# First stage of a Fourier-mixing kernel: the two ends of the first index as 64x32 tiles side by side, outputs at a pitch of 56 columns

## The chip, the cores and the metric

The kernel runs on one core of a Trainium2 chip. The metric is the device time of one execution in microseconds (us). Before the change three runs took 1851.91, 1852.71 and 1855.34 us; their median is 1852.71.

## The reference

The reference takes `x` of shape 8 x 3008 x 256 (batches, sequence, features) and two weight matrices, 256 x 2048 and 2048 x 256, all float32. It computes the real part of a two-dimensional Fourier transform of each batch and sends the 24064 rows of the result through a small network:

```python
X = np.fft.fft(x, axis=1)
X = np.fft.fft(X, axis=2)
a = X.real.reshape(8 * 3008, 256)
h = a @ w_in
g = h * (1.0 / (1.0 + np.exp(-1.702 * h)))
out = g @ w_out
```

## The kernel before, in words

The transform over the sequence of 3008 = 47 x 64 is done in two stages. The transform over the features is folded into the first weight matrix (`wcs`), so that it costs no step of its own. The rest, by far the largest part, is the network: products of 64-column halves on TensorE, with the activation between them on ScalarE and sums on VectorE and GpSimd. The steps of the network (`steps`, a batch, a block of four, a half and a pair of hidden blocks each) are written out in one loop, and what has to be done for the next batch is put between them by a table, `extra`: `at(t, fn, ...)` runs `fn` at the end of step `t`. The order on every engine is the order of this program; nothing rearranges it.

For batch b + 1 the table holds, while batch b runs through the network: the load of `x` into `xt` (`load_x`); `fold1` on GpSimd, which adds and subtracts mirrored rows and, at its first call, puts the two ends of the first index (0 and 32 of the 64 residues) into a tile `e` of their own; four calls of `mix1`, the first stage; after each of them two calls of `spill`, which write the result to `Td` in DRAM; `fill`, which reads it back with other rows; and `stage2`, which multiplies it with the matrices of the second stage in tiles of 64x32.

`mix1(b, m)` uses the array of TensorE in four quarters of 64 rows by 64 columns. Quarter (r, c) reads 47 partitions of `xt` from partition 64 r on and writes 64 partitions of a PSUM bank `ps[r]` from partition 64 c on. In each call every quarter has two matmuls of 256 columns, one per i. Each writes 48 useful rows: 24 frequencies, of each a part 0 and a part 1 in turn (NM = 48); the weights are read as windows of 64 columns at a pitch of 48, so that the last 16 rows come from the next matrix and are not used.

The one matmul with jj = 0, in quarter (0, 0) of the call with m = 0, is special. The ends have only one part each: part 0 from index 0, part 1 from index 32. It is made of four matmuls, two pieces of the columns (0 to 128 and 129 to 255) by two parts. The weights of part 0 have zeros in the columns of part 1 and the other way round, and the second of each pair adds to the first in the same 64 rows. The four quarters' matmuls are issued in an order that takes, each time, the quarter with the least work so far (`had`); an ordinary matmul counts 2 in it and one of the four end matmuls 1.

After `mix1` ScalarE copies both banks into `xt` (`mixed`, the second bank in the next step), and the spills take 48 partitions from partition 64 c on. The first batch has a first stage of its own (`mix_first`), so that `mix1` runs for seven batches.

Of the kernel before, what the change touches and what calls it, by code (L numbers as in the profile page):

```python
# [27 lines left out]
F32 = mybir.dt.float32  # L28
# [6 lines left out]
NA, NB = 47, 64  # L35
NJ = NB // 2
NM = 48
ENDS = 0, NJ, NJ + 1, NJ + 2
PIECES = (0, 32), (32, NA)
NU, NG = 2, 12  # L40
# [6 lines left out]
def view(ap, offset, *dims):  # L47
    return bass.AP(ap.tensor, ap.offset + offset, [list(d) for d in dims])
# [6 lines left out]
def kp(u, a):  # L55

    n, i = a // 4, 2 * (a % 4) + u
    return 8 * n + i if n else 7 - i


def tables(S, D):

    assert S == NA * NB and D == 256
    H = D // 2
    ks = np.array([kp(u, a) for a in range(NG) for u in range(NU)])
    s = NB * np.arange(NA)[:, None, None] + np.arange(NB)[None, :, None]
    angle = 2.0 * np.pi * ((s * ks) % S) / S
    cos, sin = np.cos(angle), np.sin(angle)
    w1 = np.zeros((NA, NJ + 3, NG * NU, 2))
    w1[:, 1:NJ, :, 0], w1[:, 1:NJ, :, 1] = cos[:, 1:NJ], sin[:, 1:NJ]  # L70
    e0, o0, e1, o1 = ENDS
    w1[:, e0, :, 0], w1[:, o0, :, 0], w1[:, e1, :, 1], w1[:, o1, :, 1] = cos[:, 0], sin[:, 0], cos[:, NJ], sin[:, NJ]


    w0 = np.zeros((128, NJ + 1, NG * NU, 2))
    low, high, back = w0[0:2 * NA:2], np.zeros((NA, NJ + 1, NG * NU, 2)), NJ - np.arange(1, NJ)
    low[:] = w1[:, :NJ + 1]
    high[:, 1:NJ, :, 0], high[:, 1:NJ, :, 1] = cos[:, NJ + back], -sin[:, NJ + back]
    high[:, e0, :, 1], high[:, o0, :, 1] = cos[:, NJ], -sin[:, NJ]
    w0[33:33 + 2 * NA:2] = high  # L80
    sign = np.ones((128, 4))
    sign[33:33 + 2 * NA:2] = -1.0

    c, q = np.divmod(np.arange(NJ), 16)
    m2 = []
    for jj in np.where(c, 16 + q, np.where(q, 16 - q, 0)), 4 * (q // 2) + 2 * (q % 2) + c:
        j, k2 = jj[:, None], np.arange(NB)[None, :]
        beta = 2.0 * np.pi * ((j * k2) % NB) / NB
        m = np.zeros((NU, 2, NJ, 2, NB))
        m[:, 0, :, 0], m[:, 1, :, 0] = np.cos(beta), -np.sin(beta)  # L90
        m[:, 0, :, 1], m[:, 1, :, 1] = np.sin(beta), np.cos(beta)
        m[:, :, 0, 0] = m[:, :, 0, 1] = np.stack([np.ones(NB), 1.0 - 2.0 * (np.arange(NB) % 2)])
        m2.append(m)
    rot = np.zeros((NU, 2, NJ, NU, 2, NJ))
    for i in range(NU):
        for n in range(NJ):
            rot[i, 0, n, i, 1, n], rot[i, 1, n, i, 0, n] = (1.0, -1.0) if n else (0.0, 0.0)
        rot[i, 0, 0, i, 0, 0] = rot[i, 1, 0, i, 1, 0] = 1.0

    m, d = np.arange(D)[:, None], np.arange(H)[None, :]  # L100
    phi = 2.0 * np.pi * ((m * d) % D) / D
    cd = np.stack([np.cos(phi), -np.sin(phi)], 1)
    cd[:, 1, 0] = 1.0 - 2.0 * (np.arange(D) % 2)
    cd = cd.reshape(2, H, 2, H).transpose(1, 0, 2, 3)
    small = [t.reshape(128, -1) for t in (*m2, rot, cd)]
    pad = 64 - NM
    w1 = np.pad(w1.reshape(NA, -1), ((0, 128 - NA), (0, pad)))
    w0 = np.concatenate([w0.reshape(128, -1), np.zeros((128, pad)), sign], 1)
    return np.concatenate([w0, w1], 1).astype(np.float32), np.concatenate(small, 1).astype(np.float32)

# [2 lines left out]
def kernel(ctx: ExitStack, tc, x, w_in, w_out, tab1, tab2, out):  # L113
    nc = tc.nc
    B, S, D = x.shape
# [6 lines left out]
    const = ctx.enter_context(tc.tile_pool(name="const", bufs=1, space=SB))  # L122
# [11 lines left out]
    Tk = nc.dram_tensor("Tk", (B * NBLK * NF, 1), F32, kind="Internal").ap()  # L134
    Td = [nc.dram_tensor(f"Td{b}", (NG * 128, D), F32, kind="Internal").ap() for b in range(B)]

    w1 = const.tile([128, (NJ + 3) * NM + 64 - NM], F32, tag="w1", name="w1")
    small = const.tile([128, 4 * NB + 128 + 4 * H], F32, tag="small", name="small")
    m2f, m2 = (small[:, i * 2 * NB:(i + 1) * 2 * NB].rearrange("p (c n) -> p c n", c=2) for i in range(2))
    rot = small[:, 4 * NB:4 * NB + 128]  # L140
# [21 lines left out]

    def mat(w, jj, rows):

        return w[rows, jj * NM:jj * NM + 64]

    spare = ["b0", "b1", "b2", "o2", "o3", "o4"]

    def bank(name, tag=None):
        if tag is None:  # L170
            tag = spare.pop(0)
            spare.append(tag)
        if tag in ("o0", "o1"):
            return o_banks[int(tag[1])]
        return (rest if tag[0] == "o" else psp).tile([128, 512], F32, tag=tag, name=name)
# [11 lines left out]
    xt = xp.tile([128, NJ, D], F32, tag="x", name="xt")  # L187
# [20 lines left out]
    e0 = {}  # L208
# [24 lines left out]
    def mix1(b, m):  # L233

        ps = [bank("ps1") for _ in range(2)]
        queues = {}
        for i in (2 * m, 2 * m + 1):
            for r in range(2):
                for c in range(2):
                    rows, o = slice(64 * r, 64 * r + NA), ps[r][64 * c:64 * c + 64, i % 2 * D:(i % 2 + 1) * D]  # L240
                    jj, todo = 4 * i + 2 * r + c, queues.setdefault((r, c), [])
                    if jj:
                        todo.append((2, o, mat(w1, jj, rows), xt[rows, 31 - (2 * i + c), :], not todo, True))
                        continue
                    for k, c0, c1 in ((0, 0, H + 1), (1, H + 1, D)):
                        for part in range(2):
                            todo.append((1, o[:, c0:c1], mat(w1, ENDS[k + 2 * part], rows), e0[b][:, part, c0:c1], not todo,
                                         part == 1))

        had = {key: 0 for key in queues}  # L250
        while any(queues.values()):
            key = min((key for key in queues if queues[key]), key=lambda key: (had[key], key))
            size, o, w, rhs, first, end = queues[key].pop(0)
            had[key] += size
            nc.tensor.matmul(o, lhsT=w, rhs=rhs, start=first, stop=end, skip_group_check=True)  # L255

        waiting.append((m, ps[1]))
        mixed(m, 0, ps[0])
# [3 lines left out]
    def mixed(m, r, ps):  # L262
        nc.scalar.copy(free(xt[:], (4 * m + r) * D, [2 * D, 2], [1, D]), free(ps[:], 0, [D, 2], [1, D]))
# [6 lines left out]
    def at_rows(first, at, *dims):  # L270
        one = xt[first:first + 1]
        return bass.AP(one.tensor, one.offset + at * D, [[2 * xt[:].ap[0][0], NM]] + [list(d) for d in dims])

    def load_first(k):

        lo, apart = 4 * k, (28 - 8 * k) * D
        nc.sync.dma_start(out=at_rows(0, lo, [apart, 2], [1, 4 * D]), in_=view(x, lo * D, [NB * D, NM], [apart, 2], [1, 4 * D]))

    def load_mirror(k):

        parts = ((1, 4), (28, 32)) if k == 0 else ((4 * k, 4 * k + 4), (28 - 4 * k, 32 - 4 * k))
        for lo, hi in parts:
            nc.scalar.dma_start(out=at_rows(33, lo, [D, hi - lo], [1, D]),
                                in_=view(x, (NB - lo) * D, [NB * D, NM], [-D, hi - lo], [1, D]))
        if k == 0:
# [50 lines left out]

    def spill(b, c, q):

        nc.sync.dma_start(out=view(Td[b], (16 * c + 4 * q) * D, [NJ * D, NM], [1, 4 * D]),
                          in_=xt[64 * c:64 * c + NM, 4 * q:4 * q + 4, :].rearrange("p q d -> p (q d)"))  # L340

    def fill(b, a0=0, a1=NG):
        if a0 == 0:
# [504 lines left out]
    for lo, hi in (28, 32), (24, 28), (20, 24), (8, 12), (12, 20):  # L848
# [8 lines left out]
                      in_=view(tab1, 0, [tab1.shape[1], 128], [28 * NM, 2], [1, ends]))  # L857
# [101 lines left out]
    for b in range(B):  # L959
# [5 lines left out]
        if b + 1 < B:  # L965
            folds, groups, filled = PLANS[min(b, 1)]
            for c in range(NCH):
                for part in range(2):
                    at(t0 + folds[2 * c + part], fold1, b + 1, c, part, nc.gpsimd)
                if c % 2:  # L970
                    k = t0 + groups[c // 2]
# [18 lines left out]
    for t in range(n + LAG):  # L990
        if t < NP:
# [32 lines left out]
            if t == NP - 1:  # L1024
                doubled(NP)
                middle(NP + 1)
        else:
            after, special = (any(fn in (mix1, stage2) for fn, _ in extra.get(k, ())) for k in (t - 1, t))
            if t < n:
                begin(t, 1)  # L1030
# [81 lines left out]
```

## Time and profile before

| | |
|---|---|
| median of 3 runs | 1852.71 us |
| the profiled execution | 1851.27 us, its span 1849.5 us |
| granted TensorE clock | 0.999 |
| busy: TensorE, VectorE, ScalarE, GpSimd | 99%, 80%, 62%, 54% |
| mean of the DMA engines | 57 GB/s |

The span reaches from the first instruction to the last; the execution's own time also has what lies around it, here 1.8 us. PE is TensorE's matmuls, PEld its weight loads, DVE VectorE, ACT ScalarE, POOL GpSimd and SP the engine that issues most transfers. In the profile each float32 matmul is two instructions MATMUL, called passes below. A form such as 47*64 gives the rows and columns of the array that are used; the groups give minimum, median and maximum in ns. The timeline's columns are the start in us, the time that the merged instructions cover in us, the engine, the line and the operation, output and inputs, the form, and how many were merged. Matmuls are pipelined, so the covered time of neighbours overlaps.

### The profile page before, as it was taken

What the parts mean: (1) busy time and instruction counts of PE and PEld (TensorE: products, weight loads), DVE (VectorE), ACT (ScalarE), POOL (GpSimd) and SP (SyncE); (2) the same over time, 40 slices, a digit from 0 to 9 for tenths busy, and PEclk for the clock granted to TensorE, in tenths of its full rate; (3) what the DMA queues carried; (4) which work ended last, traced back from release to release, by engine and by line L of the source; (5) the groups of instructions that cost most, each with busy time, mean ns of one, the idle gap of its engine ahead of it and who ended that gap; (6) DMA issues with size and microseconds to landing.
All of it is one profiled execution on the core that took longest, in us unless ns stands there. A gap on an engine that the chain in (4) does not pass through costs nothing.

```text
span 1849.5 us, 55986 instructions
## 1 busy us (share of the span) xinstructions
PE 1835.5 (99%) x23722; PEld 1411.0 (76%) x23722; DVE 1485.5 (80%) x1928; ACT 1148.6 (62%) x2241; POOL 1001.1 (54%) x1053
## 2 busy tenths in 40 slices
PE   8999999999999999999999999999999999999998
PEld 5677777777777777777777777777788777778776
DVE  6988778887888778877788778878888788878875
ACT  5666656666666666666665666666655666656663
POOL 4786456554556546565365544656446654444442
PEclk9999999999999999999999999999999999999999
DMA  8721341214211151211502115121241112100111
GB/s 285 178 61 34 87 65 28 55 32 103 44 48 40 33 112 29 60 33 48 109 13 71 33 48 97 22 72 26 71 73 23 35 26 56 30 19 13 23 19 24
DMA packets 149706, 105.31 MB, mean 57 GB/s; under 512 B 106057, under 2 KB 130665, under 8 KB 148896
## 3 DMA queue, kind: packets, MB, share of 16 engines
q1 hardware_dynamic: 146624, 99.68, 24.0%
q8 instruction: 187, 3.06, 0.7%
q10 hardware_dynamic: 2832, 2.05, 0.5%
q14 instruction: 63, 0.52, 0.1%
HBM read 64.41 MB, written 48.05 MB: 61 GB/s over the span
## 4 chain that ended last, share of the span: by engine, by line
PE 88%; DVE 8%; DMA 2%; ACT 1%; issue 1%; POOL 0%; SPq 0%; DVEq 0%; ACTq 0%; POOLq 0%
PE x L184 32%; PE o L184 25%; PE low L684 23%; PE o L684 4%; PE ps L255 2%; DVE big L650 2%; PE ps L365 1%; DVE big L622 1%; DVE big L604 1%; DVE big L786 1%; DVE big L648 1%; DVE big L646 1%; DMA xt<-in_x_dram 1%; DMA Td<-big 1%; DVE big L804 0%
## 5 line engine op out<-in xcount | busy, mean ns | idle before, releaser
L615 POOL TENSOR_TENSOR big<-big 128x256 f32<-128x256 f32 (+1 forms) x376 | 357.9, 952 | 797.0 <-ACT big L607 694.5
L184 PE MATMUL x<-pq,wcs 128*64 128x256 f32 (+1 forms) x6016 | 776.8, 376 | 1.0 <-ACT x L585 0.4
L184 PE MATMUL o<-big,wo 128*64 128x256 f32 (+1 forms) x4800 | 629.0, 375 | 0.6 <-issue 0.6
L184 PEld LDWEIGHTS x<-pq,wcs 128*64 128x64 f32 x6016 | 421.9, 137 | 175.9 <-issue 15.3
L184 PEld LDWEIGHTS o<-big,wo 128*64 128x64 f32 x4800 | 348.0, 137 | 145.9 <-issue 1.0
L597 ACT ACTIVATE g<-x 128x512 f32<-128x512 f32 (+1 forms) x376 | 221.8, 590 | 379.9 <-PE x L184 378.6
L604 DVE TENSOR_TENSOR big<-g,x 128x512 f32<-128x512 f32 (+1 forms) x376 | 250.8, 667 | 186.5 <-ACT big L600 186.4
L616 POOL TENSOR_TENSOR big<-big 128x256 f32<-128x256 f32 (+1 forms) x376 | 399.6, 1063 | 0.0
L585 ACT ACTIVATE x<-nb,af 128x256 f32<-128x256 f32 (+1 forms) x752 | 353.0, 469 | 69.1 <-DVE pq L372 55.9
L684 PE MATMUL low<-big 128*64 128x128 f32 (+1 forms) x5888 | 386.1, 270 | 0.0
L684 PEld LDWEIGHTS low<-big 128*64 128x64 f32 x5888 | 341.0, 137 | 27.9
L600 ACT ACTIVATE big<-x 128x512 f32<-128x512 f32 (+1 forms) x376 | 219.2, 583 | 123.5 <-PE x L184 113.6
L646 DVE TENSOR_TENSOR big<-big 128x1024 f32<-128x1024 f32 (+1 forms) x184 | 234.1, 1272 | 65.2 <-PE low L684 41.4
L607 ACT ACTIVATE big<-big 128x512 f32<-128x512 f32 (+1 forms) x376 | 231.7, 616 | 37.2 <-DVE big L604 35.4
L684 PE MATMUL low<-big,wo 128*64 128x128 f32 (+1 forms) x2944 | 224.8, 271 | 1.4 <-DVE big L650 0.7
L648 DVE TENSOR_TENSOR big<-big 128x512 f32<-128x512 f32 (+1 forms) x184 | 177.1, 963 | 15.9
L650 DVE TENSOR_TENSOR big<-big 128x512 f32<-128x512 f32 (+1 forms) x184 | 185.4, 1007 | 0.0
L684 PEld LDWEIGHTS low<-big,wo 128*64 128x64 f32 x2944 | 175.4, 137 | 6.4 <-DVE big L650 2.9
L622 DVE TENSOR_TENSOR big<-big 128x512 f32<-128x512 f32 (+1 forms) x188 | 140.7, 748 | 3.3 <-POOL big L615 3.3
L623 DVE TENSOR_TENSOR big<-big 128x512 f32<-128x512 f32 (+1 forms) x188 | 135.6, 721 | 6.5
L684 PEld LDWEIGHTS o<-big,wo 128*64 128x64 f32 x1472 | 94.3, 137 | 24.3
L684 PE MATMUL o<-big,wo 128*64 128x128 f32 (+1 forms) x1472 | 112.2, 270 | 0.0
(97 smaller groups left out, 1144.6 us busy)
## 6 DMA issues: line engine op xcount, KB each, us to landing
out_dram<-os SPq DMA_DIRECT2D x284, 64.0 KB
t<-Td SPq DMA_DIRECT2D x22, 512.0 KB
Td<-xt SPq DMA_DIRECT2D x56, 192.0 KB
xt<-in_x_dram SPq DMA_DIRECT2D x14, 512.0 KB
xt<-Xr SPq DMA_DIRECT2D x14, 512.0 KB
nb<-Nd SPq DMA_DIRECT2D x23, 256.0 KB
out_dram<-os SPq DMA_DIRECT2D x96, 56.0 KB
Xr<-in_x_dram SPq DMA_DIRECT2D x7, 752.0 KB
```

The lines of the kernel that those rows point to most:

```text
L184: nc.tensor.matmul(out[c0:c0 + 64], lhsT=lhs[:, c0:c0 + 64], rhs=rhs, skip_group_check=True, **how)
L585: nc.scalar.activation(x[:, i * 256:i * 256 + n], nbt[b, blk][:, hh * 256:hh * 256 + n], ACTF.Copy, scale=af1[:, f:f + 1])
L597: nc.scalar.activation(two(g[:], n), two(xb[t][:], n), ACTF.Copy, scale=2.0)
L600: nc.scalar.activation(front(t), two(xb[t][:], width(t)), ACTF.Gelu_apprx_sigmoid)
L604: nc.vector.tensor_tensor(back(t), two(gt.pop(t)[:], n), two(xb.pop(t)[:], n), op=ALU.subtract)
L607: nc.scalar.activation(back(t), back(t), ACTF.Gelu_apprx_sigmoid)
L615: eng.tensor_tensor(right(t, S1, n), left(t, A21, n), right(t, A22, n), op=ALU.add)
L616: eng.tensor_tensor(left(t, S3, n), left(t, A11, n), left(t, A21, n), op=ALU.subtract)
L646: nc.vector.tensor_tensor(free(big[:], SUM, *both_), free(big[:], from11 + w, *twice), free(big[:], from11, [at_right(t, 0) + w - from11, ...
L648: nc.vector.tensor_tensor(s2, a11, s1, op=ALU.subtract)
L650: nc.vector.tensor_tensor(s4, a12, s2, op=ALU.subtract)
L684: nc.tensor.matmul(o, lhsT=lhs, rhs=rhs, start=first_in, stop=(p == NP - 2), skip_group_check=True)
```

## The change

`PITCH` is 56: the 24 columns of part 0 come first, then 8 of zeros, then the 24 of part 1, so that part 1 begins at row 32 of a quarter. The table `w1` is laid out in this way, and windows of 64 columns are read at the new pitch. The four end matmuls take 32 columns each: part 0 writes rows 0 to 31 of the quarter, part 1 rows 32 to 63, and none adds to another. In `had` an ordinary matmul counts 4 and one of the end matmuls 1. A spill becomes two transfers of 24 partitions, one for each part, to the same places in `Td`.

```diff
+PITCH = 32 + NM // 2
...
-    w1 = np.pad(w1.reshape(NA, -1), ((0, 128 - NA), (0, pad)))
+    apart = np.zeros((NA, NJ + 3, PITCH))
+    apart[:, :, :NM // 2], apart[:, :, 32:] = w1[..., 0], w1[..., 1]
+    w1 = np.pad(apart.reshape(NA, -1), ((0, 128 - NA), (0, 64 - PITCH)))
...
-        return w[rows, jj * NM:jj * NM + 64]
+        return w[rows, jj * PITCH:jj * PITCH + 64]
...
                     if jj:
-                        todo.append((2, o, mat(w1, jj, rows), xt[rows, 31 - (2 * i + c), :], not todo, True))
+                        todo.append((4, o, mat(w1, jj, rows), xt[rows, 31 - (2 * i + c), :], not todo, True))
                         continue
                     for k, c0, c1 in ((0, 0, H + 1), (1, H + 1, D)):
                         for part in range(2):
-                            todo.append((1, o[:, c0:c1], mat(w1, ENDS[k + 2 * part], rows), e0[b][:, part, c0:c1], not todo,
-                                         part == 1))
+                            at = ENDS[k + 2 * part] * PITCH + 32 * part
+                            todo.append((1, o[32 * part:32 * part + 32, c0:c1], w1[rows, at:at + 32], e0[b][:, part, c0:c1],
+                                         k == 0, True))
...
-        nc.sync.dma_start(out=view(Td[b], (16 * c + 4 * q) * D, [NJ * D, NM], [1, 4 * D]),
-                          in_=xt[64 * c:64 * c + NM, 4 * q:4 * q + 4, :].rearrange("p q d -> p (q d)"))
+        for k in range(2):
+            at = 64 * c + 32 * k
+            nc.sync.dma_start(out=view(Td[b], (16 * c + 4 * q + NJ * k) * D, [2 * NJ * D, NM // 2], [1, 4 * D]),
+                              in_=xt[at:at + NM // 2, 4 * q:4 * q + 4, :].rearrange("p q d -> p (q d)"))
```

The tile for `w1` in SBUF grows from 1696 to 1968 columns.

More of the change, by code (lines that the diff above doesn't have):

```diff
@@ L135 @@
     Td = [nc.dram_tensor(f"Td{b}", (NG * 128, D), F32, kind="Internal").ap() for b in range(B)]
-    w1 = const.tile([128, (NJ + 3) * NM + 64 - NM], F32, tag="w1", name="w1")
+    w1 = const.tile([128, (NJ + 3) * PITCH + 64 - PITCH], F32, tag="w1", name="w1")
     small = const.tile([128, 4 * NB + 128 + 4 * H], F32, tag="small", name="small")
```

## The prediction

> **What bounds the kernel now.** I read the page first: busy shares, then the chain.
>
> ```profile
> PE 1835.5 (99%) x23722; PEld 1411.0 (76%) x23722; DVE 1485.5 (80%) x1928; ACT 1148.6 (62%) x2241; POOL 1001.1 (54%) x1053
> ...
> PE 88%; DVE 8%; DMA 2%; ACT 1%; issue 1%; POOL 0%; SPq 0%; DVEq 0%; ACTq 0%; POOLq 0%
> ```
>
> TensorE (PE) is busy 99% of 1849.5 us and carries 88% of the chain that ended last; in the view of waits its largest single wait is 2.7 us, at the start. So a change of TensorE's own time is passed on one to one, and I look for nothing else before that is settled. A matmul here is float32 and shows in the trace as two passes, each with a weight load (PEld) of its own.
>
> Next the instructions that write the first stage's PSUM tile `ps`:
>
> ```profile
> L255 PE MATMUL ps<-xt,w x434: 375/376/428, 120.2 to 1541.3; 47*64 47x256 f32 x145
> L255 PE MATMUL ps<-e,w x56: 266/269/322, 120.2 to 1429.0; 47*64 47x129 f32 x28, 47*64 47x127 f32 x28
> L365 PE MATMUL ps<-t,small x1536: 268/269/296, 31.9 to 1728.0; 64*32 64x128 f32 x192
> ```
>
> The change touches the 56 passes that read `e` (28 matmuls, four in each of seven batches) and their neighbours. Durations of single passes overlap, so I take times from starts. The timeline of one block with the ends (batch 2, m = 0), with the last matmul before and the first after it:
>
> ```profile
> 305.70 0.60 PE L184 MATMUL o<-big,wo 128*64 128x256 f32 x4
> 306.24 0.32 PE L255 MATMUL ps<-e,w 47*64 47x129 f32 x1
> 306.24 0.44 PE L255 MATMUL ps<-xt,w 47*64 47x256 f32 x3
> ...
> 306.73 0.27 PE L255 MATMUL ps<-e,w 47*64 47x127 f32 x1
> 306.73 0.38 PE L255 MATMUL ps<-xt,w 47*64 47x256 f32 x2
> 306.84 0.27 PE L255 MATMUL ps<-e,w 47*64 47x127 f32 x1
> ```
>
> and one without ends (m = 1), followed by the same work:
>
> ```profile
> 342.93 1.09 PE L255 MATMUL ps<-xt,w 47*64 47x256 f32 x16
> 343.95 0.65 PE L184 MATMUL x<-pq,wcs 128*64 128x256 f32 x4
> ```
>
> Three things to see. The four quarters of the array run side by side: an end and three ordinary passes start together at 306.24. The quarter with the ends is a chain of its own, one 128-column pass each 0.107 us (306.73, 306.84) beside ordinary 256-column passes at twice that. And the block with ends takes 1.44 us from its first start to the next work (306.24 to 307.68), the one without 1.02 (342.93 to 343.95): the ends cost 0.42 us in each of seven batches, 2.95 us in all. The reason is in the counts: quarter (0,0) has eight end passes of 0.107 and two ordinary ones of 0.215, 1.29 us; the others four of 0.215, 0.86 us.
>
> Last, what a change of tile shape costs:
>
> ```profile
> 307.38 0.38 PE L255 MATMUL ps<-xt,w 47*64 47x256 f32 x1
> 307.68 0.41 PE L184 MATMUL x<-pq,wcs 128*64 128x226 f32 x2
> ```
>
> ```profile
> 29.40 0.59 PE L335 MATMUL warm<-wcs 128*128 128x512 f32 x1
> 29.92 0.65 PE L184 MATMUL psw<-wst,small 128*64 128x512 f32 x2
> ```
>
> From 64x64 to 128x64 the next start comes 0.30 us after a pass that streams for 0.215: 0.09 lost. From 128x128 to 128x64, where only the width differs, 0.52 after a pass of 0.43: 0.09 again. I find 0.092 to 0.096 at every change of shape in the trace, stage 2's 64x32 tiles included. Behind each the first pass is longer by its weight load, which was not taken ahead as within one shape: 0.05 us for 64 columns (0.267 against 0.216), 0.03 for 32 (0.134 against 0.107).
>
> **The change, part by part.**
>
> *The ends.* Four matmuls of 64x64 become four of 64x32. Parts 0 and 1 no longer add into the same 64 rows but write rows 0 to 31 and 32 to 63. Side by side they need the time of two matmuls, four passes instead of eight: 0.43 us off quarter (0,0). That two 64x32 tiles of one quarter run together is shown by stage 2, where eight such tiles start within 0.05 us.
>
> *The order.* With the sizes 4 and 1 the sort by work done gives, for m = 0: one end; the three ordinary matmuls of the other quarters; three ends; four ordinary ones. By the shapes: 64x32, 64x64, 64x32, 64x64, three changes inside a block that before had none; those on entry and exit stay. A change between 64x64 and 64x32 is not in the trace. Its price lies between nothing (a change of tile within a shape: the next start 0.006 us later) and 0.094 plus the weight load; no row supports a gain from a change itself. I take the upper end, since all changes in the trace cost the same whichever dimension differs, and the nearest row, 128x128 to 128x64, differs in width alone, as here. A change there also means that nothing of the new shape starts before the old has drained: the weight loads, taken ahead otherwise, begin only with the first pass. So I take the four runs as one behind the other:
>
> - one end: 0.03 + 2 x 0.107 = 0.243, then 0.094
> - three ordinary, side by side: 0.05 + 2 x 0.215 + 0.01 for staggered starts = 0.493, then 0.094
> - three ends: parts 1 and 0 side by side, then part 1 of the second piece: 0.03 + 4 x 0.107 = 0.455, then 0.094
> - four ordinary, to the start of the last pass: 0.05 + 0.215 + 0.02 = 0.284
>
> Sum 1.757 us, against 1.14 now (306.24 to 307.38). That is +0.617 a batch, x7 = +4.3 us. Even at no price for the change itself, runs that exclude each other give 1.475, +0.34 a batch or +2.3 us: what decides is whether the shapes may overlap. [...]
>
> *Who waits.* Behind the block TensorE's next matmuls (L184, `x`) start later by the same time. ScalarE's copy of `ps` to `xt` (L263) ends later too, and behind it in ScalarE's queue stand the preparation of the next `x` and the activations; they wait for TensorE already (the page gives 378.6 us for L597) and move with it.
>
> *The spills.* Two issues of 48 partitions become four of 24. The queue of SP at one of them:
>
> ```profile
> 422.39 0.79 SPq L339 DMA_DIRECT2D Td<-xt  x2
> 426.21 0.22 SPq L392 DMA_DIRECT2D Tk<-big  x1
> 426.61 0.38 SPq L345 DMA_DIRECT2D t<-Td  x1
> ```
>
> 56 more issues, at L339's median of 0.41 us, are 0.8 us per group; here 3 us are free behind them, in which SP waits for the next step's work. I cost them at nothing. The read-back at 426.61 is wanted by stage 2 at 461.07, so a later landing has 30 us of cover. Without that cover 0.8 us would show once per group: 28 x 0.8 = 22 us at most; the free 3 us speak against it.
>
> *The rest at nothing.* The table grows from 1696 to 1968 columns, 0.1 MB more in four loads from 47.45 us; VectorE's and GpSimd's instructions are the same, and the first fold that needs `xt` runs at 102.6 us without a wait for a DMA.
>
> Sum: 1851.27 of the profiled execution (span 1849.5) + 4.3 = 1855.6. The median of the runs lies 1.4 above that execution, so 1857.0, +0.23%. About 0.2%, 3.7 us, can be told from no change in this kernel.
>
> **Rivals.**
>
> 1. *Shapes overlap in different cells.* Nothing drains, since ends and ordinary matmuls stand in different quarters; then all four quarters need 0.86 us and the block costs as much as one without ends: -0.42 x 7 = -2.95 us, 1849.8, -0.16%. For it: quarters already run apart from each other (306.24). Against: the weight loads that wait at every change of shape. It decides if a start of an ordinary matmul follows that of the first end by 0.01 us. [...]
> 2. *Only the quarter concerned drains.* Ends 0.455, 0.094, then 0.05 + 0.215 to the last start: 0.82 against 1.14, -0.32 x 7 = -2.3 us, 1850.4. No row tells it from rival 1, as all changes of shape in the trace hit cells in use.
> 3. *The change does not do what it says*: the two tiles of a quarter run one after the other. Two more end passes in the third run, 0.21: +0.83 x 7 = +5.8 us, 1858.5. Stage 2 speaks against it.
>
> **How the numbers follow.** Forecast 0.75, rival 1 0.14, rival 2 0.07, rival 3 0.04. In the forecast a change of shape must cost over (3.7 / 7 - 0.34) / 3 = 0.06 us to be told from nothing; with 0.09 in the rows and the scatter of the runs I give that 0.8. Slower: 0.6 + 0.04 = 0.64. Faster by over 0.2% needs more than the whole 2.95 us that the ends cost: 0.05, for scatter and what I have not seen. The same: 0.31. The forecast's own range is 1855.0 (no price for a change, +2.3) to 1858.2; the whole one reaches down to rival 1 and up to rival 3: 1849.6 to 1858.6.
>
> **What would show it.** In the timeline of a block with ends, m = 0: right, if four runs stand one behind the other, about 2.06 us pass from the first start to the next L184, and 64x32 passes never start within an ordinary run. Wrong, if ordinary matmuls start within 0.01 us of the first end and the block takes 1.02 us (rival 1) or 1.12 (rival 2). Blocks with m = 1 to 3 must keep 1.02. A wait of TensorE behind L339's transfers would show a term that I left out.

## The result, and the profile after

The changed kernel takes 1856.98 us (median of 11 runs, 1855.74 to 1858.52), the kernel before beside it 1851.91 (11 runs). The ratio is 1.0024 with a 95% interval of 1.0016 to 1.0032: slower by 3.0 to 5.9 us. The profiled execution took 1855.80 us, with a span of 1854.0, 4.5 more than before.

From the page of the changed kernel, the busy time and the chain:

```profile
PE 1839.7 (99%) x23722; PEld 1411.2 (76%) x23722; DVE 1485.7 (80%) x1928; ACT 1148.7 (62%) x2241; POOL 999.5 (54%) x1053
PE 88%; DVE 8%; DMA 2%; ACT 1%; issue 1%; POOL 0%; SPq 0%; DVEq 0%; ACTq 0%; POOLq 0%
```

As many matmuls as before, 4.2 us more busy time on TensorE, the other engines within 2 us and the chain as they were. This points to TensorE. The instructions that write `ps` (now line 259):

```profile
L259 PE MATMUL ps<-xt,w x434: 376/376/428, 120.5 to 1545.9; 47*64 47x256 f32 x145
L259 PE MATMUL ps<-e,w x56: 266/270/294, 120.2 to 1433.4; 47*32 47x129 f32 x28, 47*32 47x127 f32 x28
```

The ends have the form 47*32 now, and a single pass takes what it took (median 270 ns against 269). Neither row shows a loss; the starts do. The timeline of the block with ends in batch 2:

```profile
306.29 0.60 PE L187 MATMUL o<-big,wo 128*64 128x256 f32 x4
306.82 0.41 PE L259 MATMUL ps<-e,w 47*32 47x129 f32 x2
307.16 0.66 PE L259 MATMUL ps<-xt,w 47*64 47x256 f32 x6
307.75 0.62 PE L259 MATMUL ps<-e,w 47*32 47x129 f32 x6
308.30 0.66 PE L259 MATMUL ps<-xt,w 47*64 47x256 f32 x8
308.89 0.41 PE L187 MATMUL x<-pq,wcs 128*64 128x226 f32 x2
```

Before, rows of `e` and of `xt` took turns, since they ran side by side. Now there are four runs, one behind the other: one end (two passes), three ordinary matmuls (six), three ends (six), four ordinary ones (eight). The three ordinary matmuls stand in other quarters than the first end and still start 0.34 us after it. From the first start to the next work it is 2.07 us (306.82 to 308.89), against 1.44 before. The block without ends has not changed (before: 342.93 to 343.95); by single rows of the trace all 21 such blocks take 1.024 or 1.025 us to the next work:

```profile
344.13 1.10 PE L259 MATMUL ps<-xt,w 47*64 47x256 f32 x16
345.16 0.44 PE L187 MATMUL x<-pq,wcs 128*64 128x256 f32 x2
```

### The profile page after: what moved, and what is told of

Read it like the earlier page. It is cut to its first block, busy times and chain, and to the rows that moved or that the text cites. A ratio compares the mean times of both kernels' runs of the same rounds, so it can differ in the third digit from the quotient of the medians.

```text
span 1854.0 us, 56040 instructions
## 1 busy us (share of the span) xinstructions
PE 1839.7 (99%) x23722; PEld 1411.2 (76%) x23722; DVE 1485.7 (80%) x1928; ACT 1148.7 (62%) x2241; POOL 999.5 (54%) x1053
## 4 chain that ended last, share of the span: by engine, by line
PE 88%; DVE 8%; DMA 2%; ACT 1%; issue 1%; POOL 0%; SPq 0%; DVEq 0%; ACTq 0%; POOLq 0%
PE x L187 32%; PE o L187 25%; PE low L690 23%; PE o L690 4%; PE ps L259 2%; DVE big L656 2%; PE ps L371 1%; DVE big L628 1%; DVE big L610 1%; DVE big L792 1%; DMA xt<-in_x_dram 1%; DVE big L654 1%; DVE big L652 1%; DMA Td<-big 0%; DVE big L810 0%
```

## The experiments

The theory, from the starts above: in a block, tiles of one shape run at a time. A pass of another shape starts only about 0.09 us after the last pass of the old shape has streamed, in whichever quarter that stands (the first ordinary pass 0.34 us after the start of the first end), and it is longer by its weight load (0.05 us for 64 columns, 0.03 for 32). The rivals: the loss comes from the spills or the larger table; only the quarter concerned waits; two tiles of one quarter do not run at once. Four kernels were measured on one chip, beside 27 runs of the kernel before (median 1852.46 us); the ratios and differences below are against these. Times from first to last start are from single rows of the trace.

### The ends ahead of everything else

```diff
-                            todo.append((1, o[32 * part:32 * part + 32, c0:c1], ...
+                            todo.append((0, o[32 * part:32 * part + 32, c0:c1], ...
```

> The four end matmuls are issued ahead of the seven ordinary ones: one change of shape inside a block instead of three; all else as after the change. Theory (runs of different shape exclude each other, 0.094 us a change): 0.03 + 4 x 0.107 = 0.46 for the ends, 0.094, then 0.72 to the start of the last pass: 1.27 us against 1.14 before and 1.76 after the change. +0.13 x 7 = +0.9 us on before (+0.05%), 3.4 us less than the changed kernel. Rival (the shapes overlap, and the loss of the changed kernel lies in its spills or its table): the block takes as long as with the order of the changed kernel, and the time stays at +4 to +5 us.

Measured: 1853.69 us, ratio 1.0004 (0.9996 to 1.0013), +1.2 us by the medians, which is not clear of the kernel before. The timeline of its block:

```profile
307.47 0.63 PE L259 MATMUL ps<-e,w 47*32 47x129 f32 x8
308.03 1.09 PE L259 MATMUL ps<-xt,w 47*64 47x256 f32 x14
309.06 0.98 PE L187 MATMUL x<-pq,wcs 128*64 128x226 f32 x8
```

Two runs, and 1.59 us from first start to next work; first to last start is 1.28, where 1.27 was expected. The ends, the spills and the table are those of the changed kernel; the order alone takes back most of the loss (3.3 us by the medians).

### The ends as before, the layout and the spills as after

```diff
-                            at = ENDS[k + 2 * part] * PITCH + 32 * part
-                            todo.append((1, o[32 * part:32 * part + 32, c0:c1], w1[rows, at:at + 32], ..., k == 0, True))
+                            todo.append((1, o[:, c0:c1], mat(w1, ENDS[k + 2 * part], rows), ..., not todo, part == 1))
...
-                        todo.append((4, o, mat(w1, jj, rows), ...
+                        todo.append((2, o, mat(w1, jj, rows), ...
```

> The ends are 64x64 tiles that add into the same rows again, in the order and with the sizes of before; the pitch of 56, the larger table and the spills in two transfers stay. Theory: these cost nothing, so the time is that of before within 1 us, and the block with ends takes 1.14 us from first to last start. Rival (the doubled spills or the table are part of the cost): up to the whole +4 to +5 us of the changed kernel remains.

Measured: 1852.89 us, ratio 1.0002 (0.9993 to 1.0011), +0.4 us by the medians. First to last start is 1.14 us, as before. The doubled spills and the larger table cost nothing that can be told; the runs alone leave room for 2.0 us. Its profiled execution, with a span of 1855.0 us, shows why spans of single executions do not settle such a question:

```profile
L187 PE MATMUL x<-pq,wcs x6016: 354/379/431, 81.6 to 1836.7; 128*64 128x256 f32 x162, 128*64 128x226 f32 x33
```

Its first `x` matmul starts at 81.6 us, those of the kernel before and of the changed one at 75.9: the whole 5.5 us by which its span is longer than that of before lie in the start-up, ahead of any block in question. Without the start-up the traces do compare: from the start of the first block with ends to the last instruction this kernel takes 1729.14 us, the kernel before 1729.26 and the changed kernel 1733.83. So the spills and the table, which this kernel shares with the changed one, do not show here either.

### The old order with the new tiles: five changes of shape

```diff
-                        todo.append((4, o, mat(w1, jj, rows), ...
+                        todo.append((2, o, mat(w1, jj, rows), ...
```

> The changed kernel with the sizes 2 and 1 in the order, as before: one end, three ordinary, two ends, three ordinary, one end, one ordinary, which makes five changes of shape instead of three. Theory: 0.243 + 0.493 + 0.247 + 0.493 + 0.241 + 0.265 = 1.98, and five changes at 0.094 give 2.45 us to the last start, +1.31 x 7 = +9.2 us on before (+0.5%). Rival (the order does not matter, since only the quarter concerned drains): as the changed kernel, +4 to +5 us.

Measured: 1862.31 us, ratio 1.0048 (1.0034 to 1.0062) from five runs, +9.9 us by the medians. The timeline:

```profile
312.08 0.41 PE L259 MATMUL ps<-e,w 47*32 47x129 f32 x2
312.42 0.66 PE L259 MATMUL ps<-xt,w 47*64 47x256 f32 x6
313.00 0.41 PE L259 MATMUL ps<-e,w 47*32 47x129 f32 x4
313.34 0.66 PE L259 MATMUL ps<-xt,w 47*64 47x256 f32 x6
313.93 0.40 PE L259 MATMUL ps<-e,w 47*32 47x127 f32 x2
314.26 0.64 PE L259 MATMUL ps<-xt,w 47*64 47x256 f32 x2
314.83 0.41 PE L187 MATMUL x<-pq,wcs 128*64 128x226 f32 x2
```

Six runs, 2.75 us to the next work; 2.44 from first to last start (2.45 expected), 1.30 more than before, in seven batches 9.1 us. The ends and the ordinary matmuls are those of the changed kernel and of the first experiment; one, three and five changes of shape give 1.28, 1.76 and 2.44 us. Not all of this growth is the price of the changes, since shorter runs also leave more quarters idle: by the sums of the expectations and the prediction the runs alone need 1.18, 1.48 and 1.98 us. What is left is 0.10, 0.29 and 0.46 us, 0.09 to 0.10 for each change.

### The whole block in one shape

```diff
...
-                        todo.append((4, o, mat(w1, jj, rows), xt[...], not todo, True))
...
+                    for k in range(2 if m == 0 else 1):
+                        todo = queues.setdefault((r, c, k), [])
+                        if jj:
+                            o_, w = (o, mat(w1, jj, rows)) if m else (
+                                o[32 * k:32 * k + 32], w1[rows, jj * PITCH + 32 * k:jj * PITCH + 32 * k + 32])
+                            todo.append((2, o_, w, xt[...], not todo, True))
...
```

> In the calls with m = 0 every ordinary 64x64 matmul is written as two of 64x32 side by side, so that the whole block has one shape; ends, layout and spills as after the change. Theory: no change of shape is left inside, the two ends of a quarter run side by side and each of the eight tiles has 0.86 us of work: 0.03 + 3 x 0.215 + 0.05 for staggered starts = 0.72 to the last start against 1.14 before, -0.42 x 7 = -2.9 us (-0.16%), the gain that the first rival of the prediction gave. Rival (two tiles of one quarter do not run at once, or the doubled number of instructions holds TensorE up): no gain; in series the block needs twice 0.86 us and the time is +4 us or more.

Measured: 1849.32 us, ratio 0.9983 (0.9974 to 0.9992), -3.1 us by the medians: faster than the kernel before by 0.17% (0.08% to 0.26%), and so faster than the changed one. The timeline, where `e` and `xt` take turns again:

```profile
307.17 0.30 PE L262 MATMUL ps<-e,w 47*32 47x129 f32 x2
307.19 0.43 PE L262 MATMUL ps<-xt,w 47*32 47x256 f32 x6
307.31 0.39 PE L262 MATMUL ps<-e,w 47*32 47x129 f32 x4
307.43 0.41 PE L262 MATMUL ps<-xt,w 47*32 47x256 f32 x6
307.53 0.27 PE L262 MATMUL ps<-e,w 47*32 47x127 f32 x2
307.64 0.63 PE L262 MATMUL ps<-xt,w 47*32 47x256 f32 x16
308.20 0.98 PE L187 MATMUL x<-pq,wcs 128*64 128x226 f32 x8
```

It is 1.02 us to the next work by single rows (307.172 to 308.196), what a block without ends takes. The kernel issues 98 more passes (23820 on its page against 23722), and they cost nothing that shows, since the second tile of a pair runs beside the first. The two ends of quarter (0, 0) start 0.006 us apart, and all eight tiles within 0.05 us. So two 64x32 tiles of one quarter run at once, and ends and ordinary matmuls overlap here when they have one shape.

## Why the prediction was right, point by point

- *TensorE bounds, and its time is passed on one to one.* Seven blocks with 0.62 us more each are 4.3 us; the span grew by 4.5, the busy time of PE by 4.2. In the other direction the last experiment saved 0.42 us a block, 2.9 us, with 3.1 measured (1.5 to 4.8 by its interval). From the start of the first block to the last instruction, where the start-up is left out, the traces give +0.8 us for the first experiment (7 blocks: +1.0), +9.2 for the third (+9.1) and -2.7 for the last (-2.9).
- *The ends run side by side.* Right, by the last experiment; in the changed kernel itself the gain is there too, inside the third run (six passes in 0.55 us with its change of shape, 307.75 to 308.30) and is outweighed.
- *A change between 64x64 and 64x32 costs what the others do.* This was the term with the widest bounds. In the changed kernel the last ordinary pass of the second run and the next end start 0.306 us apart (307.440 and 307.746 as single rows of the trace) after a stream of 0.215: 0.09 lost. At the two other changes of the block, 0.200 and 0.196 us from start to start behind passes that stream for 0.107, it is 0.09 as well. The value came from 128x128 to 128x64, which differs in width alone, and it held. The prediction's "every change of shape in the trace" is a little too wide: a few changes behind passes of one or four columns, or with a wait in them, lose 0.12 us or more (in the trace of before the next start comes 0.121 to 0.165 us behind a pass of one column and 0.129 behind one of four). None of them enters the sum.
- *Shapes exclude each other across the array.* Right: four runs, predicted at 1.757 us from first to last start and measured at 1.761 in six of the seven batches and 1.762 in the last. It holds term by term, each run with the change behind it: 0.337, 0.587, 0.549 and 0.284 predicted, 0.335, 0.586, 0.553 and 0.287 measured in batch 2. (Three terms of the prediction are up to 0.003 us off what their own figures add up to; this cancels to 0.001.) Of the 0.62 us, by the prediction's terms, 0.28 are the three changes of shape and 0.34 the lost overlap. That split was worked out and not measured by itself, since no kernel here has the runs without the price of the changes; the three orders, with 0.09 to 0.10 us left for each change, agree with it.
- *The rivals.* Overlap in different cells and a drain of the quarter alone both fall by the same two rows: ordinary matmuls of other quarters wait for the first end (306.82, 307.16). A series of the two tiles falls by the last experiment, and already in the changed kernel, where the first two ends of the third run start 0.007 us apart (307.746 and 307.753).
- *The spills at nothing.* Right, by the second experiment, and in TensorE's waits none is behind them. SP's queue at the place shown before:

```profile
423.60 1.89 SPq L345 DMA_DIRECT2D Td<-xt  x4
427.42 0.21 SPq L398 DMA_DIRECT2D Tk<-big  x1
427.86 0.39 SPq L351 DMA_DIRECT2D t<-Td  x1
```

Here the four issues take 1.89 us against 0.79 for two, 1.1 more where 0.8 was forecast, and 1.9 us stay free behind them. This place is one of the longer ones: over the 28 groups the median went from 0.79 to 1.54 us, 0.75 more, and all 112 issues together take 21 us more than the 56 did (44.2 against 23.2), where 22 was forecast.

- *The chance of no measurable difference.* The forecast of 4.3 us lay close to the 3.7 that the prediction took to be the least that can be told apart, and the interval, 3.0 to 5.9, still reaches below it. The medians differ by 5.1, and the ratio of 1.0024 stands for 4.4; the traces, from the first block on, differ by 4.6. What lies beyond the 4.3 of the blocks is within the scatter of the runs.
- *The time itself.* That 1857.0 was forecast and 1856.98 measured is luck to this degree: the forecast built on a median of 1852.71 from three runs, while 11 runs of the same kernel have 1851.91 and the 27 later ones 1852.46. What was predicted well is the 0.62 us in the block.

## What to carry to other kernels

Before smaller tiles are put beside larger ones, count the changes of shape in the order in which the matmuls are issued: here each held back the whole array (ordinary matmuls of the other quarters started 0.34 us after the first end), and its price, 0.09 us, could be read from places in the trace of before where another shape changed already. A block in which everything has the smaller shape, at the cost of more instructions, kept the overlap and was the fastest of all here (1849.32 us); where two shapes are needed, put each into one run, as the first experiment did (1.28 us from first to last start against 1.76). And compare starts, not durations: the rows of single passes looked the same in the faster and in the slower kernel (medians of 269 and 270 ns).

## What the runs showed of the hardware that was not expected

The prediction did not look at writing the ordinary matmuls in the smaller shape too. Cutting each 64x64 matmul into two 64x32 cost no time here: a block with 36 passes on eight tiles took the same 0.72 us from first to last start as one with 16 passes on four. And the start-up, ahead of the first `x` matmul, varied from 75.9 us (the changed kernel) to 81.6 (the second experiment) between profiled executions whose start-up is the same program, more than the 4.3 to 5.1 us of the effect studied. The spread over runs, the times within blocks and the time from the first block to the end were of use; the spans of single executions were not.
